# The key-value sums of pairs 0 to 7, with the exponentials as the stationary operand

## The chip, the cores and the metric

The kernel runs on one core of one Trainium2 chip. The metric is device time in microseconds, lower is better. Three runs of the kernel before gave 1171.79, 1172.33 and 1173.0 us; the median, 1172.33 us, is the time before.

In the profile the engines are called PE (matrix unit), PEld (its weight load, which overlaps PE), DVE (vector), ACT (scalar, activations), POOL (general purpose) and SP (queue of transfers).

## The reference

An attention with a feature map (8 batches, 8 heads, 576 positions, 64 values each) feeds a two-layer network. What is computed:

```python
def phi(x):
    proj = np.einsum('bhsd,df->bhsf', x, w_phi)                 # 64 -> 128 features
    proj = proj - np.max(np.abs(proj), axis=-1, keepdims=True)
    return np.concatenate([np.exp(proj), np.exp(-proj)], axis=-1)  # 256 features
q_p, k_p = (phi(q), phi(k))
kv = np.einsum('bhsf,bhsd->bhfd', k_p, v)
z = np.sum(k_p, axis=2)
num = np.einsum('bhsf,bhfd->bhsd', q_p, kv)
den = np.einsum('bhsf,bhf->bhs', q_p, z)[..., None] + 1e-06
attn = num / den
x = attn.transpose(0, 2, 1, 3).reshape(4608, 512)
h = x @ w_in                                                     # 512 -> 2048
out = np.maximum(0.01 * h, h) @ w_out                            # 2048 -> 512
```

All of it is fp32. The part that the change touches is `kv` and `z`: for each head a sum over the 576 positions of the 256 exponentials of a key times the 64 values of that position, and of the exponentials alone.

## The kernel before

**Pairs.** The 64 heads are worked on in 32 pairs. A pair has a key phase (projection, largest absolute value, subtraction, two exponentials, key-value sums) and a query phase (the same for the queries, then the product with the sums, then the division). A pair's 576 positions are taken in 5 chunks: four of 128 positions and one of 64, which sits on partitions 64 to 127.

**Two precisions.** Pairs 0 to 7 use plain fp32 matmuls. Each plain fp32 matmul of the program appears in the trace as two MATMUL records and two LDWEIGHTS records. Pairs 8 to 31, and the two layers of the network, split each operand in a high and a low part and use three faster matmuls in place of one (the type is F32R); these are one record each.

**Key-value sums of pairs 0 to 7.** For each chunk and each of the two heads one matmul has the 66 columns of the values as the stationary operand (64 values and two columns of ones, tile `rv`) and the 256 exponentials of the chunk as the moving operand (tile `e` in `first_k_phase`, `ek` in `k_phase`). The five chunks add up in one PSUM bank, `kvp`, 66 partitions by 2 x 256. The query phase wants the sums the other way round, features on the partitions. So the bank is copied to SBUF by ACT (`kvs`, L480 and L327, where the helper at L68 records it), turned by four transposes on PE into another bank (`kvt`, L485 and L333), and copied from there to `kvh` by two ACT copies: the 64 sums, and the column of `z` spread over 64 columns (L487 and L488, L336 and L337).

**Stages.** Pairs 0 and 1, then 2 and 3, run through `first_k_phase` (L445), then their queries through `first_q_phase` (L508) in three units of columns. Pairs 4 to 7 run through `k_phase` (L219) and `q_phase`, between matmuls of the network's layers for the first two blocks of 256 tokens (`layer1` L607, `layer2` L622). Meanwhile the weights of the two layers come in, 32 pieces, and DVE, ACT and POOL split them (`load_weights`, L170 to L200). From pair 8 on, attention of the next batches runs between the layers of the blocks before. The last blocks have layers alone.

**What sets the order.** The program gives each piece a priority, and a scheduler at build time, which plays the program through with its own idea of each instruction's duration, writes a fixed order for each engine. On the chip each engine takes its instructions in that order, and a waiting instruction holds back all behind it on its engine. PSUM banks come in four groups: `a` (3), `c` (1), `h` (2), `acc` (2). The sums of pairs 0 to 3 stand in `h`, those of pairs 4 to 7 in `c`, and all turned sums in `c`.

Of the kernel before, what the change touches and what calls it, by code (L numbers as in the profile page):

```python
# [45 lines left out]
def attention_moe_kernel(ctx: ExitStack, tc: tile.TileContext, q, k, v, w_phi, w_in, w_out, out):  # L46
# [171 lines left out]

    def k_phase(i):  # L219
# [62 lines left out]
        def chunk(c):  # L282
# [3 lines left out]
            if nat:  # L286
                nc.scalar.activation(ek[r, :, 0:F], pmk[r, 2 * s : 2 * s + 2], AF.Exp)
                nc.scalar.activation(ek[r, :, F:256], pmk[r, 2 * s : 2 * s + 2], AF.Exp, scale=-1.0)
                for j in range(2):
                    kv_mm(j, rv[r, 4 * j + c if c < 4 else 8 + j], ek[r, j], first=c == 0, last=c == 4)  # L290
                return
# [32 lines left out]
        if nat:  # L324
            load_v(i + 1)
        kvs = st([P, 2, 256], F32, "kk", "kvs").rearrange("p a (b f) -> p a b f", b=2)[0:66]
# [7 lines left out]
        if i < NN:  # L334
            kvh = st([P, 2, 2, P], F32, "kvh")
            nc.scalar.copy(kvh[:, :, :, 0:64], kvtv[:, :, :, 0:64])  # L336
            nc.scalar.copy(kvh[:, :, :, 64:P], kvtv[:, :, :, 64:65].broadcast_to([P, 2, 2, 64]))  # L337
            kvs_of[i] = kvh, None
        else:
            kvh = st([P, 2, 2, P], F32R, "kvh")  # L340
            kvl = st([P, 2, 2, P], F32R, "kvl")
            zb = kvtv[:, :, :, 64:65].broadcast_to([P, 2, 2, 64])
            copy_("kvh", kvh[:, :, :, 0:64], kvtv[:, :, :, 0:64])
            copy_("kvh", kvh[:, :, :, 64:P], zb)
            nc.vector.tensor_tensor(kvl[:, :, :, 0:64], kvtv[:, :, :, 0:64], kvh[:, :, :, 0:64].bitcast(F32), op=ALU.subtract)
            nc.vector.tensor_tensor(kvl[:, :, :, 64:P], zb, kvh[:, :, :, 64:P].bitcast(F32), op=ALU.subtract)
            kvs_of[i] = kvh, kvl
# [97 lines left out]
    def first_k_phase(i):  # L445
# [7 lines left out]
        for g in range(3):  # L453
# [18 lines left out]
            for s in range(w):  # L472
                c = 2 * g + s
                for j in range(2):
                    nc.tensor.matmul(kvp[0:66, 256 * j : 256 * j + 256], lhsT=rv[r, 4 * j + c if c < 4 else 8 + j],  # L475
                                     rhs=e[r, 2 * s + j].rearrange("p t f -> p (t f)"),
                                     start=c == 0 and j == 0, stop=c == 4, skip_group_check=True)
                yield
        kvs = st([P, 2, 256], F32, "kk", "kvs").rearrange("p a (b f) -> p a b f", b=2)[0:66]
# [247 lines left out]
```

## Time and profile before

| | before |
|---|---|
| median of 3 runs | 1172.33 us (1171.79 to 1173.0) |
| the profiled execution's own time | 1170.85 us |
| span of its trace | 1169.1 us |
| granted PE clock | 1.00 of full speed in the whole |
| busy: PE, PEld, DVE, ACT, POOL | 98%, 88%, 64%, 73%, 56% |

The span is what the trace shows from the first instruction to the last; 1.75 us of the execution lie outside. "Busy" of PE is taken from modelled ends of overlapping matmuls, so the pace of matmuls is better read from the starts of two groups that follow each other than from the length of one.

### The profile page before, as it was taken

How to read it: one execution, taken by the hardware profiler on the slowest of the kernel's cores; microseconds unless marked ns; L12 is line 12 of the kernel's file. 1: busy time of each engine (PE TensorE's matmuls, PEld its weight loads, DVE VectorE, ACT ScalarE, POOL GpSimd, SP SyncE). 2: the span in 40 equal slices, each digit the busy share in tenths (PEclk: the TensorE clock that was granted, in tenths of full speed). 3: DMA queues.
4: the chain of work that ended last, by engine and by line, in shares of the span. 5: the costliest groups of instructions: out<-in, count | busy, mean ns of one | idle time of the engine just before them, and what ended most of it. 6: DMA issues, size and time to landing. Idle time of an engine off the chain costs nothing.

```text
span 1169.1 us, 21456 instructions
## 1 busy us (share of the span) xinstructions
PE 1144.0 (98%) x7496; PEld 1025.8 (88%) x7496; DVE 751.6 (64%) x1316; ACT 856.2 (73%) x2256; POOL 649.1 (56%) x702
## 2 busy tenths in 40 slices
PE   8899999999999999999999999999999999999998
PEld 5677778898998999989999999999999999999997
DVE  6878996677778777776787777757867675200000
ACT  5878786888887888878888788868888885433232
POOL 1451222567667676767666766767666665533232
PEclk9999999999999999999999999999999999999999
DMA  8425441211111111111111111101111100000000
GB/s 221 151 78 153 123 119 36 66 37 33 52 34 51 34 41 33 44 31 32 42 34 52 33 52 26 49 22 41 34 51 34 41 2 20 1 19 10 10 19 19
DMA packets 69980, 57.87 MB, mean 50 GB/s; under 512 B 52208, under 2 KB 53488, under 8 KB 69872
## 3 DMA queue, kind: packets, MB, share of 16 engines
q1 hardware_dynamic: 67120, 55.78, 16.9%
q8 instruction: 59, 0.97, 0.4%
q10 hardware_dynamic: 2752, 0.72, 0.3%
q14 instruction: 49, 0.40, 0.1%
HBM read 46.27 MB, written 9.44 MB: 48 GB/s over the span
## 4 chain that ended last, share of the span: by engine, by line
PE 73%; DVE 12%; ACT 8%; issue 3%; DMA 2%; SPq 1%; POOL 1%; DVEq 0%; ACTq 0%; POOLq 0%
PE h L610 9%; PE h L613 9%; PE h L611 9%; PE acc L632 9%; PE acc L630 9%; PE acc L631 9%; PE c L241 6%; PE a L418 2%; PE a L423 2%; PE a L264 2%; PE a L420 2%; DVE tq L395 1%; DVE ql L189 1%; DMA m<-m 1%; PE h L475 1%
## 5 line engine op out<-in xcount | busy, mean ns | idle before, releaser
L73 POOL TENSOR_TENSOR gl<-g,gh 128x256 fp32r<-128x256 f32 x288 | 234.8, 819 | 321.4 <-ACT gh L68 242.4
L610 PE MATMUL h<-xh,w0h 128*128 128x256 f32 x1088 | 277.1, 282 | 2.8 <-ACT g L617 1.3
L611 PE MATMUL h<-xh,w0l 128*128 128x256 f32 x1088 | 275.5, 280 | 0.0
L610 PEld LDWEIGHTS h<-xh,w0h 128*128 128x128 f32 x1088 | 204.6, 188 | 13.6 <-ACT g L617 2.8
L630 PE MATMUL acc<-w1h,gh 128*128 128x512 f32 x544 | 214.2, 394 | 0.1
L631 PE MATMUL acc<-w1l,gh 128*128 128x512 f32 x544 | 213.4, 392 | 0.0
L611 PEld LDWEIGHTS h<-xh,w0l 128*128 128x128 f32 x1088 | 204.5, 188 | 8.4
L632 PE MATMUL acc<-w1h,gl 128*128 128x512 f32 x544 | 203.3, 394 | 0.2 <-POOL gl L73 0.2
L613 PE MATMUL h<-xl,w0h 128*128 128x256 f32 x1088 | 189.6, 280 | 0.1
L617 ACT ACTIVATE g<-h 128x256 f32<-128x256 f32 x288 | 108.6, 381 | 98.1 <-PE h L613 79.7
L73 POOL TENSOR_TENSOR ql<-eq,qh 128x576 fp32r<-128x576 f32 x96 | 144.4, 1517 | 41.9 <-DVE qh L409 29.1
L68 ACT CAST gh<-g 128x256 fp32r<-128x256 f32 x288 | 115.2, 402 | 67.8 <-PE acc L631 66.1
L613 PEld LDWEIGHTS h<-xl,w0h 128*128 128x128 f32 x1088 | 155.1, 188 | 1.2 <-POOL xl L73 0.5
L73 POOL TENSOR_TENSOR kpl<-ek,kph 128x512 fp32r<-128x512 f32 x72 | 99.6, 1383 | 75.4 <-ACT kph L68 65.4
L70 DVE COPY o<-acc 128x512 f32<-128x512 f32 x17 | 11.7, 686 | 162.8 <-DMA out_dram<-o 77.9
L632 PEld LDWEIGHTS acc<-w1h,gl 128*128 128x128 f32 x544 | 99.7, 188 | 15.9 <-POOL gl L73 0.6
L630 PEld LDWEIGHTS acc<-w1h,gh 128*128 128x128 f32 x544 | 102.3, 188 | 12.3 <-ACT gh L68 0.4
L631 PEld LDWEIGHTS acc<-w1l,gh 128*128 128x128 f32 x544 | 102.3, 188 | 11.3
L294 ACT ACTIVATE ek<-pmk,m4n 128x128 f32<-128x128 f32 (+1 forms) x240 | 90.2, 392 | 12.1 <-DVE m4n L278 8.5
L295 ACT ACTIVATE ek<-pmk,m 128x128 f32<-128x128 f32 (+1 forms) x240 | 89.6, 390 | 8.0 <-DVE m L272 7.0
L269 DVE TENSOR_TENSOR pmk<-a,pmk 128x256 f32<-128x256 f32 (+1 forms) x120 | 49.4, 419 | 58.4 <-ACT pmk L68 56.9
L409 DVE TENSOR_REDUCE qh<-eq 128x576 fp32r<-128x576 f32 x96 | 69.0, 750 | 24.0 <-ACT eq L403 21.7
(186 smaller groups left out, 2399.5 us busy)
## 6 DMA issues: line engine op xcount, KB each, us to landing
out_dram<-o SPq DMA_DIRECT2D x36, 256.0 KB, 2.1
rv<-in_v_dram SPq DMA_DIRECT2D x28, 320.0 KB, 3.6
rq<-in_q_dram SPq DMA_DIRECT2D x28, 288.0 KB, 3.0
rk<-in_k_dram SPq DMA_DIRECT2D x27, 288.0 KB, 2.8
ring<-in_w_in_dram SPq DMA_DIRECT2D x9, 512.0 KB, 3.6
f<-in_w_out_dram SPq DMA_DIRECT2D x7, 512.0 KB, 3.7
f<-in_w_in_dram SPq DMA_DIRECT2D x7, 512.0 KB, 3.7
ring<-in_w_out_dram SPq DMA_DIRECT2D x5, 512.0 KB, 4.3
```

What stands on the lines that cost most here:

```text
L68: nc.scalar.copy(o, i)
L73: (nc.vector if pick(key) == "v" else nc.gpsimd).tensor_tensor(o, a, b, op=op)
L241: nc.tensor.matmul(kvp[0 : lt.shape[1], 256 * j : 256 * j + 256], lhsT=lt, rhs=rt, start=first and j == 0, stop=last, skip_group_check=True)
L294: nc.scalar.activation(ek[r, j, 0:F], pmk[r, h], AF.Exp, bias=m4n[r, h : h + 1])
L295: nc.scalar.activation(ek[r, j, F:256], pmk[r, h], AF.Exp, scale=-1.0, bias=m4[r, h : h + 1])
L610: nc.tensor.matmul(ph, lhsT=weight(0, "h", ft)[:, d * P : d * P + P], rhs=xh[d], start=d == 0, stop=False)
L611: nc.tensor.matmul(ph, lhsT=weight(0, "l", ft)[:, d * P : d * P + P], rhs=xh[d], start=False, stop=False)
L613: nc.tensor.matmul(ph, lhsT=weight(0, "h", ft)[:, d * P : d * P + P], rhs=xl[d], start=False, stop=d == NP - 1)
L617: nc.scalar.activation(g, ph, AF.Prelu, alpha=0.01)
L630: nc.tensor.matmul(a, lhsT=gh[:, ts], rhs=weight(1, "h", ft), start=ft == 0, stop=False)
L631: nc.tensor.matmul(a, lhsT=gh[:, ts], rhs=weight(1, "l", ft), start=False, stop=False)
L632: nc.tensor.matmul(a, lhsT=gl[:, ts], rhs=weight(1, "h", ft), start=False, stop=ft == NFT - 1)
```

## The change

In pairs 0 to 7 the two operands of the key-value matmuls change places. For each chunk and head there are now two matmuls, one for each half of the 256 features: the 128 exponentials are stationary and the 66 columns of `rv` move (`kv_nat`). The sums come out with the features on the partitions, four blocks of 66 columns in one bank. So the copy to `kvs` and the four transposes are gone, and the two copies to `kvh` read the bank of the sums itself (`kv_copy`). Pairs 8 to 31 keep their code.

```diff
+    def kv_nat(kvp, rv, r, c, ek):
+        for j in range(2):
+            for t in range(2):
+                n = 66 * (2 * j + t)
+                nc.tensor.matmul(kvp[:, n : n + 66], lhsT=ek(j, t), rhs=rv[r, 4 * j + c if c < 4 else 8 + j],
+                                 start=c == 0 and n == 0, stop=c == 4, skip_group_check=True)
+
+    def kv_copy(kvp, kvh):
+        kv = kvp[:, 0:264].rearrange("p (a b f) -> p a b f", a=2, b=2)
+        nc.scalar.copy(kvh[:, :, :, 0:64], kv[:, :, :, 0:64])
+        nc.scalar.copy(kvh[:, :, :, 64:P], kv[:, :, :, 64:65].broadcast_to([P, 2, 2, 64]))
+        return kvh
...
@@ k_phase: chunk
-                for j in range(2):
-                    kv_mm(j, rv[r, 4 * j + c if c < 4 else 8 + j], ek[r, j], first=c == 0, last=c == 4)
+                kv_nat(kvp, rv, r, c, lambda j, t: ek[r, j, F * t : F * t + F])
...
@@ k_phase: end
         if nat:
             load_v(i + 1)
+            kvs_of[i] = kv_copy(kvp, st([P, 2, 2, P], F32, "kvh")), None
+            yield
+            return
...
@@ first_k_phase
             for s in range(w):
-                c = 2 * g + s
-                for j in range(2):
-                    nc.tensor.matmul(kvp[0:66, 256 * j : 256 * j + 256], lhsT=rv[r, 4 * j + c if c < 4 else 8 + j],
-                                     rhs=e[r, 2 * s + j].rearrange("p t f -> p (t f)"),
-                                     start=c == 0 and j == 0, stop=c == 4, skip_group_check=True)
+                kv_nat(kvp, rv, r, 2 * g + s, lambda j, t: e[r, 2 * s + j, t])
                 yield
-        kvs = st([P, 2, 256], F32, "kk", "kvs").rearrange("p a (b f) -> p a b f", b=2)[0:66]
-        copy_("kvs", kvs, kvp[0:66].rearrange("p (a b f) -> p a b f", a=2, b=2))
-        kvt = pt("c")
-        kvtv = kvt[:, 0:264].rearrange("p (a b f) -> p a b f", a=2, b=2)
-        for j in range(2):
-            for t in range(2):
-                nc.tensor.transpose(kvtv[:, j, t], kvs[:, j, t], ident[0:66, 0:66])
-        kvh = first_kvh(i)
-        nc.scalar.copy(kvh[:, :, :, 0:64], kvtv[:, :, :, 0:64])
-        nc.scalar.copy(kvh[:, :, :, 64:P], kvtv[:, :, :, 64:65].broadcast_to([P, 2, 2, 64]))
-        kvs_of[i] = kvh, None
+        kvs_of[i] = kv_copy(kvp, first_kvh(i)), None
         yield
```

With other instructions the scheduler writes another order. Two places of it follow. (L223 is the new matmul, L228 and L229 the two copies to `kvh`; in the changed program L439 has become L448, L463 L472, L287 and L288 have become L300 and L301, and L617 has become L612. The tiles `f_79` and `f_82` hold keys and values of pairs 2 and 3, `f_80` those of pair 1, `f_81` and `ring` exponentials, `rk` the keys and `rv` the values of pair 0.)

PE in the first 25 us, key-value sums of pairs 0 and 1 and projections of pairs 2 and 3, before:

```order
L475 MATMUL h<-ring,rv 66x256 x4
L475 MATMUL h<-ring,f_80 66x256 x4
L439 MATMUL acc<-bd,f_79 128x256 x2
L439 MATMUL a<-bd,f_82 128x256 x4
L475 MATMUL h<-f_81,rv 66x256 x3
L475 MATMUL h<-ring,f_80 66x256 x2
L475 MATMUL h<-f_81,rv 66x256
L475 MATMUL h<-ring,f_80 66x256 x2
L475 MATMUL h<-ring,rv 66x256 x2
L439 MATMUL acc<-bd,f_79 128x256 x3
L439 MATMUL a<-bd,f_82 128x256
L475 MATMUL h<-f_81,f_80 66x256 x2
```

The same place in the changed program, from the last sums of chunks 2 and 3 on:

```order
L223 MATMUL h<-rv,f_81 128x66 x3
L223 MATMUL h<-f_80,ring 128x66 x4
L223 MATMUL h<-rv,ring 128x66 x4
L223 MATMUL h<-f_80,f_81 128x66 x4
L448 MATMUL acc<-bd,f_79 128x256
L448 MATMUL a<-bd,f_82 128x256 x2
L448 MATMUL acc<-bd,f_79 128x256 x2
L448 MATMUL a<-bd,f_82 128x256 x3
L448 MATMUL acc<-bd,f_79 128x256
L223 MATMUL h<-f_79,ring 128x66 x8
```

Before, six of the ten projections of pairs 2 and 3 stood after the first eight sums of pairs 0 and 1; now one stands among these sums and nine behind the last of them.

ACT after the last exponentials of pair 4 (`w0h` and `kvl` belong to the weights, `g` is the activation of layer 1), before:

```order
L186 ACTIVATE ql<-f_79 128x512
L68 COPY kvs<-c 66x512
L287 ACTIVATE ek<-pmk 128x2x128
L288 ACTIVATE ek<-pmk 128x2x128
L287 ACTIVATE ek<-pmk 128x2x128
L288 ACTIVATE ek<-pmk 128x2x128
L287 ACTIVATE ek<-pmk 128x2x128
L288 ACTIVATE ek<-pmk 128x2x128
L68 CAST w0h_92<-ql 128x512
L191 ACTIVATE kvl<-f_79 128x512
L617 ACTIVATE g<-h 128x256
L336 COPY kvh<-c 128x4x64
```

The same place in the changed program:

```order
L300 ACTIVATE ek<-pmk 128x2x128
L301 ACTIVATE ek<-pmk 128x2x128
L300 ACTIVATE ek<-pmk 128x2x128
L301 ACTIVATE ek<-pmk 128x2x128
L228 COPY kvh<-c 128x4x64
L229 COPY kvh<-c 128x4x64
L300 ACTIVATE ek<-pmk 128x2x128
L301 ACTIVATE ek<-pmk 128x2x128
L68 CAST w0h_92<-ql 128x512
L191 ACTIVATE kvl<-f_79 128x512
L612 ACTIVATE g<-h 128x256
```

The copy that needs pair 4's finished sums stood ahead of the six exponentials of pair 5; the copies that now need them stand behind six of these, and `g` has the two copies to `kvh` ahead of it, which it had behind it.

More of the change, by code (lines that the diff above doesn't have):

```diff
@@ L333, in k_phase @@
                 nc.tensor.transpose(kvtv[:, j, t], kvs[:, j, t], ident[0:66, 0:66])
-        if i < NN:
-            kvh = st([P, 2, 2, P], F32, "kvh")
-            nc.scalar.copy(kvh[:, :, :, 0:64], kvtv[:, :, :, 0:64])
-            nc.scalar.copy(kvh[:, :, :, 64:P], kvtv[:, :, :, 64:65].broadcast_to([P, 2, 2, 64]))
-            kvs_of[i] = kvh, None
[L339 to L347, printed above, removed]
+        kvh = st([P, 2, 2, P], F32R, "kvh")
+        kvl = st([P, 2, 2, P], F32R, "kvl")
+        zb = kvtv[:, :, :, 64:65].broadcast_to([P, 2, 2, 64])
+        copy_("kvh", kvh[:, :, :, 0:64], kvtv[:, :, :, 0:64])
+        copy_("kvh", kvh[:, :, :, 64:P], zb)
+        nc.vector.tensor_tensor(kvl[:, :, :, 0:64], kvtv[:, :, :, 0:64], kvh[:, :, :, 0:64].bitcast(F32), op=ALU.subtract)
+        nc.vector.tensor_tensor(kvl[:, :, :, 64:P], zb, kvh[:, :, :, 64:P].bitcast(F32), op=ALU.subtract)
+        kvs_of[i] = kvh, kvl
         yield
@@ L472, in first_k_phase @@
             for s in range(w):
-                c = 2 * g + s
-                for j in range(2):
-                    nc.tensor.matmul(kvp[0:66, 256 * j : 256 * j + 256], lhsT=rv[r, 4 * j + c if c < 4 else 8 + j],
-                                     rhs=e[r, 2 * s + j].rearrange("p t f -> p (t f)"),
-                                     start=c == 0 and j == 0, stop=c == 4, skip_group_check=True)
-                yield
-        kvs = st([P, 2, 256], F32, "kk", "kvs").rearrange("p a (b f) -> p a b f", b=2)[0:66]
-        copy_("kvs", kvs, kvp[0:66].rearrange("p (a b f) -> p a b f", a=2, b=2))
-        kvt = pt("c")
-        kvtv = kvt[:, 0:264].rearrange("p (a b f) -> p a b f", a=2, b=2)
-        for j in range(2):
-            for t in range(2):
-                nc.tensor.transpose(kvtv[:, j, t], kvs[:, j, t], ident[0:66, 0:66])
-        kvh = first_kvh(i)
-        nc.scalar.copy(kvh[:, :, :, 0:64], kvtv[:, :, :, 0:64])
-        nc.scalar.copy(kvh[:, :, :, 64:P], kvtv[:, :, :, 64:65].broadcast_to([P, 2, 2, 64]))
-        kvs_of[i] = kvh, None
+                kv_nat(kvp, rv, r, 2 * g + s, lambda j, t: e[r, 2 * s + j, t])
+                yield
+        kvs_of[i] = kv_copy(kvp, first_kvh(i)), None
         yield
```

## The prediction

> **What bounds the kernel now.** First the page's head, then the busy time by stage (columns: stretch in us, its length, busy us and instructions of each engine, granted clock, share of the transfer engines).
>
> ```profile
> span 1169.1 us, 21456 instructions
> PE 1144.0 (98%) x7496; PEld 1025.8 (88%) x7496; DVE 751.6 (64%) x1316; ACT 856.2 (73%) x2256; POOL 649.1 (56%) x702
> 5.00:41.00 36.00, 34.75 (x161) 24.56 (x162) 28.02 (x49) 24.27 (x51) 8.43 (x8) 1.00 0.75 213
> 41.00:82.00 41.00, 35.35 (x187) 27.73 (x186) 36.37 (x71) 31.54 (x77) 24.87 (x29) 1.00 0.33 99
> 82.00:100.00 18.00, 16.74 (x94) 12.75 (x94) 11.72 (x25) 12.89 (x32) 2.89 (x4) 1.00 0.53 142
> 100.00:180.00 80.00, 77.22 (x430) 61.98 (x429) 77.43 (x141) 64.76 (x149) 18.84 (x21) 1.00 0.43 123
> 180.00:400.00 220.00, 216.39 (x1448) 195.40 (x1447) 158.59 (x273) 178.55 (x483) 134.10 (x143) 1.00 0.15 41
> 400.00:980.00 580.00, 578.54 (x3998) 535.12 (x3997) 423.00 (x731) 479.39 (x1299) 392.76 (x394) 1.00 0.13 36
> ```
>
> From 180 us on PE sets the pace: 1.5 us idle in 580. Until 41 us (pairs 0 to 3) it does nearly so too. From 41 to 82 us (queries of pairs 0 to 3) PE is idle 5.7 us and DVE, at 36.4 of 41, is the tighter engine. From 100 to 180 us both are at 97%. There the question is whether PE waits for the weights that DVE splits. The waits of PE over the whole span answer it (columns: us in total, times, longest):
>
> ```profile
> PE h L610 <- ACT g L617: 3.4, 7, 1.3
> PE c L241 <- DVE kst L309: 1.7, 4, 0.9
> PE c L552 <- ACT dn L556: 1.6, 2, 1.3
> PE a L530 <- DVE pm L524: 1.6, 4, 0.5
> PE c L485 <- ACT kvs L68: 0.8, 1, 0.8
> PE h L610 <- POOL w1h L195: 0.3, 1, 0.3
> ```
>
> PE has one wait of 0.3 us on a weight tile. So the full DVE of 100 to 180 us is not what PE waits for, and PE work saved from 82 us on is time saved, as long as no other wait grows. From 41 to 82 us it may be lost to DVE.
>
> **The matmuls.** What a group costs PE is read from its start to the start of the next group, in the timeline:
>
> ```profile
> 27.82 0.41 PE L485 MATMUL c<-ident,kvs 66*128 66x66 f32 x4
> 28.07 1.89 PE L475 MATMUL h<-f,f 128*66 128x256 f32 x8
> 77.25 2.00 PE L552 MATMUL c<-eq,f 128*128 128x64 f32 x16
> 79.08 0.70 PE L376 MATMUL a<-rq,bd 128*128 128x288 f32 x2
> 80.73 1.89 PE L552 MATMUL c<-eq,f 128*128 128x64 f32 x16
> 82.43 0.36 PE L610 MATMUL h<-qh,w0h 128*128 128x256 f32 x1
> 83.70 3.62 PE L241 MATMUL c<-ek,rv 128*66 128x256 f32 x16
> 87.15 0.65 PE L376 MATMUL a<-rq,bd 128*128 128x288 f32 x2
> ```
>
> Old: 16 records in 87.15 - 83.70 = 3.45 us, 0.216 us each. A pair has 5 chunks x 2 heads x 2 records = 20, so 4.31 us.
>
> New: twice as many matmuls, 40 records a pair, each with 128 stationary columns (there were 66) and 66 moving (there were 256). No such matmul of kv is in the trace, but L552 has plain fp32 records of 128 stationary and 64 moving columns: 1.83 us / 16 = 0.114 and 1.70 / 16 = 0.106 us. I take their mean, 0.110: 4.40 us a pair. The moving side falls to a quarter, the pace only to half. Over 8 pairs this is +0.7 us, with the two rows as ends -0.5 to +2.0 us. A far lower end is the transposes, which also have 128 stationary and 66 moving columns, at 0.25 / 4 = 0.062 us; L552 is nearer, since it multiplies.
>
> [...]
>
> Gone: four transposes a pair, 0.25 us, so -2.0 us over 8 pairs. **PE work in all: +0.7 - 2.0 = -1.3 us**, half of it in pairs 0 to 3 and half in pairs 4 to 7.
>
> **The copies.** ACT loses the copy to `kvs`; the two copies to `kvh` keep their size.
>
> ```profile
> L68 ACT COPY kvs<-c 66x512 f32<-66x512 f32 x4 | 2.3, 578 | 2.1 <-PE c L241 2.1
> L68 ACT COPY kvs<-h 66x512 f32<-66x512 f32 x4 | 2.2, 589 | 0.0
> ```
>
> That is 8 copies, 4.5 us of ACT, by itself worth nothing: ACT is at 31.5 of 41 and 64.8 of 80 where they ran. If ACT had no room, they would be worth up to 4.5 us. What counts is two waits around them. No transfer changes in number.
>
> **The first wait, pairs 0 to 3.** The first row below is PE held by the copy, with the next products behind the transposes.
>
> ```profile
> 38.45 0.47 PE L485 MATMUL c<-ident,kvs 66*128 66x66 f32 x4 [0.80 <-ACT kvs L68]
> 11.40 1.89 PE L475 MATMUL h<-ring,rv 128*66 128x256 f32 x8
> 15.71 1.89 PE L439 MATMUL a<-bd,f 128*128 128x256 f32 x8
> 17.44 1.46 PE L475 MATMUL h<-f,rv 128*66 128x256 f32 x6
> 15.91 0.69 DVE L463 TENSOR_REDUCE m<-acc 128x4 f32<-128x512 f32 x1 [1.50 <-PE acc L439]
> 16.71 0.69 DVE L465 TENSOR_TENSOR pm<-acc,m 128x512 f32<-128x512 f32 x1
> 21.14 0.63 ACT L470 ACTIVATE ring<-pm 128x512 f32<-128x512 f32 x1 [1.18 <-issue]
> 21.39 0.98 DVE L189 SCALAR_TENSOR_TENSOR ql<-ring,ql 128x512 int32<-128x512 int32 x1
> 21.68 0.61 ACT L471 ACTIVATE ring<-pm 128x512 f32<-128x512 f32 x1
> ```
>
> The 0.8 us go, and with half of the PE work (-0.65) pairs 0 to 3 would end 1.45 us sooner. Against it stands the new order of projections. Nine of the ten for pairs 2 and 3 now come after all sums of pairs 0 and 1: from the first sum at 11.4 us, 40 new matmuls of 0.22 and one projection of 0.43 (four of them, 8 records, take 17.44 - 15.71 = 1.73) give 20.6 us, so DVE starts on pair 2 at about 21 instead of 15.9. Behind the projection that starts it, PE still has 8 others, 3.4 us; the chain that the first new sum of pair 2 waits for is 0.69 + 0.69 + 0.63 + 0.61 = 2.6 us. So it is just covered, unless a piece of weight work on DVE (the 0.98 us of L189) stands in between. And what PE gains meets DVE, which has 4.6 us of slack from 41 to 82. Bounds: -1.45 us (all kept) to +2.1 us, the reduction twice and the subtraction once (2.06 us) that DVE had done by 21 us and now has not, if none of it is caught up. I take -0.9: most is kept, DVE eats a third.
>
> **The second wait, pair 4.** On ACT the copy to `kvs` blocks for 2.14 us, with six exponentials of pair 5, then the weight pieces, then `g`, behind it; PE's next layer 1 waits for `g`, whose bank it needs.
>
> ```profile
> 89.90 0.58 ACT L68 COPY kvs<-c 66x512 f32<-66x512 f32 x1 [2.14 <-PE c L241]
> 90.39 0.42 ACT L287 ACTIVATE ek<-pmk 128x256 f32<-128x256 f32 x1
> 92.24 0.60 ACT L68 CAST w0h<-ql 128x512 fp32r<-128x512 f32 x1
> 92.75 0.67 ACT L191 ACTIVATE kvl<-f 128x512 int32<-128x512 uint32 x1
> 93.31 0.37 ACT L617 ACTIVATE g<-h 128x256 f32<-128x256 f32 x1
> 93.74 0.39 PE L610 MATMUL h<-qh,w0h 128*128 128x256 f32 x1 [1.26 <-ACT g L617]
> ```
>
> Now the six exponentials (92.24 - 90.39 = 1.85 us) fit in the 2.14 us of waiting. The two copies to `kvh` and two exponentials, about 1.2 us, then take the place of `kvs` and the six, 0.5 + 1.85 us, ahead of the weights and `g`: `g` starts some 1.2 us sooner, and PE's 1.26 us nearly vanish. Bounds: -1.26 to 0, if another engine's wait takes its place. I take -1.2. Pairs 4 to 7 add their half of the PE work, -0.65.
>
> **Sum:** -0.9 - 1.2 - 0.65 = -2.75 us on the profiled execution of 1170.85 us (1.75 us more than its span). The median is 1.5 us above that execution; applied to it, 1172.33 - 2.75 = **1169.6 us**.
>
> **What the sum can't hold.** From 180 us on, the work is unchanged but its order is written anew. There PE idles 3.6 us until 400 and 1.5 until 980, in single waits such as this one:
>
> ```profile
> 355.22 0.68 PE L241 MATMUL c<-kst,vhl 128*64 128x256 f32 x4 [0.89 <-DVE kst L309]
> ```
>
> Two or three such waits more or fewer give the forecast its own spread, +-2.5 us: 1167.1 to 1172.1.
>
> **The rivals.**
>
> *Nothing comes of it.* Pairs 0 to 3 end sooner but DVE sets the end of 41 to 82 us, and the 1.2 us at 93 us become a wait for the maxima of pair 4's queries. Left are -0.65 us of PE work: 1171.7. For it speaks DVE's 36.4 of 41; against it that PE has no large wait between 100 and 180 us.
>
> *The moving side sets the pace.* If a new record cost what a transpose of that shape does, 0.062 us, a pair's sums would take 2.5 us instead of 4.31: -14.6 us over 8 pairs, and -16.6 with the transposes. Pairs 0 to 3 would lose most of theirs to DVE, so I count half: 1172.3 - 8.3 - 1.2 = 1162.8. Against it stand both L552 groups. [...]
>
> *Slower: the late projections.* DVE begins on pair 2 five us later and is the tight engine until 82 us. If the lost 2.06 us are not caught up, and weight work in front of the exponentials of pairs 2 and 3 holds PE 1 us at each of two groups, the first stage ends 2.06 + 2 = 4.1 us later; with -1.85 from pair 4 on this is +2.2: 1174.5. It decides from the point where DVE's delay exceeds the 1.45 us that pairs 0 to 3 gain. For it: DVE waits 1.5 us for a projection already. Against: DVE's 4.6 us of slack, and idle time elsewhere before 41 us.
>
> **Chances.** Forecast 0.50, nothing 0.22, moving side 0.06, late projections 0.17, some other growth of waits 0.05. What a measurement of this kernel can tell from no change is about 0.2%, 2.3 us, so the bounds are 1170.0 and 1174.7. A bit over half of the forecast's half (0.28), the moving side and a little of "nothing" through the order's spread (0.06) are faster: 0.40. Slower are half of the late projections, other waits and an unlucky order: 0.18. Within: 0.42. The range, 1165.5 to 1175.0, leaves out the moving side and the worst of the late projections.
>
> **What would show it.** In the changed profile: groups of L223 at 0.106 to 0.114 us a record (0.062: the moving side). No wait of PE on a copy near 38 us. PE's last sums of pairs 2 and 3 done a microsecond or more before 38.45 us, where PE now leaves its wait for the copy. `L612` at about 92 us, with the wait of PE's next L605 below 0.3 us. The start of the last L552-like group of 64 columns (L547) before 80.7 us; if it is later, the late projections won. PE busy from 180 to 980 us within 2 us of 795. The prediction is wrong if a group of L223 runs at another pace, or if PE's idle time after 180 us moves by more than 3 us.

## The result and the profile after

The change made the kernel slower: 1181.18 us (four runs, 1177.29 to 1185.54), against 1172.41 us for the kernel before on the same chip. The ratio is 1.0072, with a 95% interval of 1.0057 to 1.0086, so about 8.8 us were lost where 2.75 were to be gained. The profiled execution took 1177.29 us, 6.4 more than the one of before. Four single runs far above all others of their kernel (1605.58 us of the kernel before, 1250.02, 3997.18 and 1444.07 us in the experiments) count in no figure of this document.

First the head of the page and the busy time by stage after the change (columns as in the prediction).

```profile
span 1175.5 us, 21728 instructions
PE 1145.8 (97%) x7624; PEld 1040.1 (88%) x7624; DVE 763.5 (65%) x1316; ACT 853.9 (73%) x2248; POOL 650.0 (55%) x702
41.00:82.00 41.00, 33.86 (x175) 26.66 (x174) 36.36 (x72) 32.18 (x77) 24.89 (x29) 1.00 0.34 99
82.00:100.00 18.00, 18.00 (x135) 16.63 (x135) 14.99 (x30) 14.21 (x34) 3.55 (x5) 1.00 0.56 170
180.00:400.00 220.00, 213.34 (x1424) 192.27 (x1423) 158.34 (x273) 176.88 (x478) 135.28 (x140) 1.00 0.15 41
400.00:980.00 580.00, 576.19 (x3956) 530.13 (x3955) 432.11 (x725) 473.76 (x1287) 384.73 (x389) 1.00 0.13 36
```

From 82 to 100 us PE now has no idle time at all (1.3 us before). But from 180 to 980 us, where the instructions are the same as before, PE is busy 789.5 us instead of 794.9.

Some of the waits of PE over the whole span, after (columns: us in total, times, longest):

```profile
PE a L525 <- DVE pm L519: 2.2, 2, 1.6
PE c L254 <- DVE kst L321: 2.0, 3, 1.3
PE c L547 <- ACT dn L551: 1.7, 1, 1.7
PE acc L627 <- POOL gl L73: 1.5, 2, 1.2
PE a L427 <- DVE pmk L282: 1.2, 1, 1.2
```

The first and third of these rows lie in the stage before 82 us. The other three are waits of layer and attention work, on the keys (`kst`), the low half of the layer's activation (`gl`) and the maximum of a key (`pmk`); `gl` and `pmk` held PE for no row of this size before.

Now the places the prediction named, in the timeline of after (columns: start, length, engine, line, operation, tiles, shape, count; in brackets the wait ahead of a row and what ended it).

```profile
11.34 1.90 PE L223 MATMUL h<-rv,ring 128*128 128x66 f32 x16
13.07 1.95 PE L223 MATMUL h<-f,ring 128*128 128x66 f32 x16
14.85 0.39 PE L223 MATMUL h<-rv,f 128*128 128x66 f32 x2
28.03 0.41 PE L223 MATMUL h<-f,ring 128*128 128x66 f32 x2 [0.91 <-issue]
37.16 0.66 PE L525 MATMUL a<-ident,pm 128*128 128x128 f32 x4
81.55 1.90 PE L547 MATMUL c<-eq,f 128*128 128x64 f32 x16
92.36 0.36 ACT L612 ACTIVATE g<-h 128x256 f32<-128x256 f32 x1
93.29 0.28 PE L605 MATMUL h<-qh,w0h 128*128 128x256 f32 x1
```

A record of the new sums costs 1.73 / 16 = 0.108 and 1.78 / 16 = 0.111 us. PE waits 0.91 us ahead of the row at 28.03. The profile names nothing that ended this wait; the exponentials on ACT just ahead of it end at 27.94, and they hang on the late projections. PE has done the sums of pairs 2 and 3 by 37.16 us, when the row behind them starts. The kernel before had done its own sums by 36.95, with only the transposes behind the wait for the copy:

```profile
36.95 0.70 PE L439 MATMUL acc<-bd,ks 128*128 128x256 f32 x2
```

So the 1.3 us between 37.16 and the end of that wait, 38.45, are not a gain. The last 64-column group of the first stage starts at 81.55 us, 0.82 later than before: by 82 us nothing of a gain is left. `g` starts 0.95 us sooner and the next L605 does not wait for it.

How far ahead is the changed kernel? I compared, from the two traces, when each has the same amount of PE work still ahead of it. By this count, which depends a little on what a record is taken to cost, the changed kernel leads by 0.9 us at 41 us, lies 0.5 behind at 82, leads by 2.3 at 120, 2.7 at 200 and 2.2 at 220. Then it is 1.1 behind at 400, 5.2 behind at 500, 3.5 at 900, and 6.3 from 980 us to the end. So the loss arises behind 220 us, most of it by 500 us, and it is larger than what was gained up to there.

The lead of 2.7 us at 200 us is not all it seems. The same group of layer 1 and the same DVE group of the attention beside it, before:

```profile
204.20 0.64 PE L613 MATMUL h<-xbl,w0h 128*128 128x256 f32 x4
205.15 0.76 DVE L269 TENSOR_TENSOR pmk<-a,pmk 128x256 f32<-128x256 f32 x2
```

And after:

```profile
201.12 0.64 PE L608 MATMUL h<-xbl,w0h 128*128 128x256 f32 x4
205.34 0.76 DVE L282 TENSOR_TENSOR pmk<-a,pmk 128x256 f32<-128x256 f32 x2
```

PE has run 3.1 us ahead with layer work, but the chain of DVE on the next keys is not ahead (0.2 us behind). PE's lead is work done early, which it lacks later as cover for that chain.

What an order can cost shows near 490 us. POOL splits the activation of layer 1 into `gl`, and PE's layer 2 needs two such pieces. After the change the second `gl` stands behind a piece of `vhl` and one of `ring`:

```profile
489.12 0.73 POOL L73 TENSOR_TENSOR gl<-g,gh 128x256 fp32r<-128x256 f32 x1
489.81 1.83 POOL L73 TENSOR_TENSOR vhl<-rv,vhl 128x512 fp32r<-128x512 f32 x2
491.72 0.79 POOL L73 TENSOR_TENSOR ring<-ring,dn 128x288 f32<-128x288 f32 x1
492.47 0.72 POOL L73 TENSOR_TENSOR gl<-g,gh 128x256 fp32r<-128x256 f32 x1
493.24 0.73 PE L627 MATMUL acc<-w1h,gl 128*128 128x512 f32 x2 [1.18 <-POOL gl L73]
```

Before, the same pieces stood with both `gl` ahead of `ring` and `vhl`, and PE did not wait (other rows of POOL stand between these):

```profile
481.35 0.74 POOL L73 TENSOR_TENSOR gl<-g,gh 128x256 fp32r<-128x256 f32 x1
483.43 0.73 POOL L73 TENSOR_TENSOR gl<-g,gh 128x256 fp32r<-128x256 f32 x1
485.51 0.80 POOL L73 TENSOR_TENSOR ring<-ring,dn 128x288 f32<-128x288 f32 x1
486.27 1.84 POOL L73 TENSOR_TENSOR vhl<-rv,vhl 128x512 fp32r<-128x512 f32 x2
486.17 0.71 PE L632 MATMUL acc<-w1h,gl 128*128 128x512 f32 x2
```

This work has nothing to do with the change. The scheduler, which plays the program through with its own durations, came out at other choices. That is the theory the experiments start from: **the new order of the unchanged work behind 220 us is what costs.** The rivals: the new arithmetic costs it (matmuls, operands, clock), or the shifted instruction stream does.

### The profile page after: what moved, and what is told of

It reads as the page before. It is cut to its first block, busy times and chain, and to the rows that moved or that the text cites. A ratio compares the mean times of both kernels' runs of the same rounds, so it can differ in the third digit from the quotient of the medians.

```text
span 1175.5 us, 21728 instructions
## 1 busy us (share of the span) xinstructions
PE 1145.8 (97%) x7624; PEld 1040.1 (88%) x7624; DVE 763.5 (65%) x1316; ACT 853.9 (73%) x2248; POOL 650.0 (55%) x702
## 4 chain that ended last, share of the span: by engine, by line
PE 76%; DVE 8%; ACT 8%; issue 3%; POOL 2%; DMA 2%; SPq 0%; ACTq 0%; DVEq 0%; POOLq 0%
PE h L605 10%; PE h L608 9%; PE h L606 9%; PE acc L627 9%; PE acc L626 9%; PE acc L625 9%; PE c L254 5%; PE a L427 2%; PE a L277 2%; PE a L432 2%; PE a L429 2%; PE h L223 2%; DVE tq L404 1%; PE a L387 1%; PE a L388 1%
## 5 line engine op out<-in xcount | busy, mean ns | idle before, releaser
L605 PE MATMUL h<-xh,w0h 128*128 128x256 f32 x1088 | 276.9, 282 | 2.1 <-ACT g L612 1.0
L605 PEld LDWEIGHTS h<-xh,w0h 128*128 128x128 f32 x1088 | 204.5, 188 | 11.1 <-ACT g L612 2.2
L612 ACT ACTIVATE g<-h 128x256 f32<-128x256 f32 x288 | 107.8, 380 | 99.1 <-PE h L608 80.1
```

Of the source, the lines that this page charges most:

```text
L605: nc.tensor.matmul(ph, lhsT=weight(0, "h", ft)[:, d * P : d * P + P], rhs=xh[d], start=d == 0, stop=False)
L612: nc.scalar.activation(g, ph, AF.Prelu, alpha=0.01)
```

## Experiments: order or arithmetic

A table of instructions for each engine can fix the order at build time. Each neighbour in the table gets a dependency on the one ahead of it on the same engine, which adds no wait between engines:

```diff
+        for line in table:                 # one line per engine
+            for earlier, later in zip(line, line[1:]):
+                tc.add_manual_dep(ins[later], ins[earlier].name, nosync, reason="order")
```

I call the order that the scheduler gives the changed kernel order A, and that of the kernel before order B. Behind the first fifth of the program they share only 74% of the neighbours on PE, 56% on ACT, 58% on DVE and 53% on POOL.

**Old arithmetic, order A behind 210 us.** The sums of pairs 0 to 7 are computed as before; only the order of what follows is that of the changed kernel.

> The mirror of the first: the arithmetic of the kernel before, its own order up to its 14th product with xbl (210.0 us), and from there what is left in the changed kernel's order. Order theory: the loss without the change, 1172.4 + 8.5 = 1181 us, between 1178 and 1185, with single runs some us apart as in the changed kernel. Arithmetic theory: 1172 to 1173. A broken fit: 1174 to 1178.

Measured: 1181.05 us, ratio 1.0072 (1.006 to 1.0084). That is the whole loss, without one instruction of the change. The busy time from 220 to 500 us, for before, after and this kernel in turn (same columns as above):

```profile
220.00:400.00 180.00, 176.59 (x1208) 160.85 (x1207) 136.40 (x236) 150.56 (x406) 119.05 (x120) 1.00 0.16 44
400.00:500.00 100.00, 99.75 (x695) 92.43 (x694) 73.69 (x133) 84.91 (x233) 68.23 (x70) 1.00 0.16 43
```

```profile
220.00:400.00 180.00, 173.92 (x1191) 158.09 (x1190) 137.56 (x237) 150.65 (x404) 117.81 (x115) 1.00 0.16 44
400.00:500.00 100.00, 98.06 (x663) 88.54 (x662) 76.81 (x126) 80.30 (x223) 66.58 (x70) 1.00 0.15 40
```

```profile
220.00:400.00 180.00, 174.25 (x1180) 158.62 (x1179) 135.55 (x234) 148.78 (x401) 118.82 (x118) 0.99 0.16 44
400.00:500.00 100.00, 98.05 (x660) 88.40 (x659) 75.56 (x126) 79.73 (x219) 65.68 (x69) 1.00 0.14 36
```

PE idles 3.7 us in this stretch before, 8.0 after, and 7.7 with the old arithmetic in order A. Idle time holds some 4 us of the loss. The rest lies within what counts as busy: PE's busy time in the whole span rose by 1.8 us (1144.0 to 1145.8), although the records cost no more. I did not break that part down further.

**New arithmetic, order B all through.** Where the two differ, the new matmuls take the places of the old ones.

> All of the changed kernel's arithmetic in the order of the kernel before from the first instruction to the last: two new matmuls stand in the place of each old one, the copies to kvh where they stood, the copies to kvs and the transposes are gone. This takes the late projections away too. Order theory: 1172.4 less 1.3 us of PE work and at most the two waits (0.9 + 1.2): 1169 to 1171 us. Arithmetic theory: 1179 to 1182.

Measured: 1173.98 us, ratio 1.0006 (0.9998 to 1.0015), 12 runs. The loss is gone, but so is the gain. The timeline shows where the two removed waits went:

```profile
26.64 1.97 PE L223 MATMUL h<-f,ring 128*128 128x66 f32 x16 [0.61 <-issue]
45.12 0.70 PE L547 MATMUL h<-eq,f 128*128 128x256 f32 x2 [1.12 <-ACT eq L532]
96.25 4.70 PE L223 MATMUL c<-rv,ek 128*128 128x66 f32 x32 [1.76 <-ACT kvl L191]
```

The wait at 45.12 has a counterpart before:

```profile
44.50 0.70 PE L552 MATMUL h<-eq,f 128*128 128x256 f32 x2 [0.90 <-ACT eq L537]
```

Times here are counted from the first sum, 12.19 us in this trace and 11.40 before. PE loses 0.61 us at 26.64 to a wait that was not there before and that the profile does not explain. It arrives only 0.4 us sooner at the queries' exponentials, which come 0.2 us sooner, so the wait there grows from 0.90 to 1.12. At the second place PE passes `g` without a wait, arrives sooner at the next pair's sums and waits 1.76 us there, behind a weight piece on ACT. What it waits for had not become faster.

**New arithmetic and order A to 214 us, order B behind.** This puts the early part of the changed kernel, with its lead of 2.2 us, ahead of the old tail.

> All of the changed kernel's arithmetic. Every engine issues the changed kernel's own order up to its 15th product with xbl (214.1 us in its trace) and from there what is left in the order of the kernel before; the orders are forced by dependencies between neighbours on one engine, which add no wait between engines. Order theory (the sums themselves give what was predicted, about -2.2 us by 220 us, and the +8.5 us of PE idle time from 220 to 980 us come from the order alone): 1170.2 us, between 1168.5 and 1172, and PE busy again as before from 400 to 980 us (579 of 580). Arithmetic theory (the new sums themselves bring the loss, whatever the order behind them): 1179 to 1182. A fit of head and tail that the swap breaks: 1174 to 1178.

Measured: 1177.67 us, ratio 1.0044 (1.0025 to 1.0063), but spread from 1172.26 to 1184.7. The tail runs parallel to that of before. So the order was right as a cause, yet this kernel should then have been at 1170 to 1173 and only its best run was. The runs' times follow their mean granted clock: 1172.26 at 1.000, 1184.7 at 0.990, some 1.2 us for 0.001. A second cause was at work, and it has its own section below.

**Which half of the change flips the order?** Pairs 4 to 7 alone changed, then pairs 0 to 3 alone, each with the order that the scheduler gives it.

```diff
 first_k_phase (pairs 4 to 7 alone):
-                kv_nat(kvp, rv, r, 2 * g + s, lambda j, t: e[r, 2 * s + j, t])
+                for j in range(2):
+                    nc.tensor.matmul(kvp[0:66, 256 * j : 256 * j + 256], lhsT=rv[r, ...], rhs=e[r, 2 * s + j]...)
 k_phase (pairs 0 to 3 alone):
-                kv_nat(kvp, rv, r, c, lambda j, t: ek[r, j, F * t : F * t + F])
+                for j in range(2):
+                    kv_mm(j, rv[r, ...], ek[r, j], first=c == 0, last=c == 4)
```

> Only pairs 4 to 7 have the new sums, pairs 0 to 3 the old; the scheduler writes the order of everything anew. By the predicted terms alone 1172.4 - 0.65 - 1.2 = 1170.5 us. Order theory: the terms hold until about 180 us, and the time is that plus what the newly written order happens to cost, anything from 1167 to 1183; PE idle time behind 220 us tells which. If the loss hangs on the sums of pairs 4 to 7: 1179 to 1182, and if it hangs on those of pairs 0 to 3 or on their late projections: 1170 to 1171.

> Only pairs 0 to 3 have the new sums; the scheduler is free, and from 220 us on it writes the order of the kernel before, instruction for instruction. Order theory: no loss behind 220 us; the time is that of the kernel before but for what pairs 0 to 3 bring, predicted -0.9 (with late projections +2.1), and what the lead table of the changed kernel shows at 82 us, +0.5: 1172 to 1174 at full clock. If the loss came from the sums of pairs 0 to 3 or their late projections: 1178 or more.

Measured: pairs 4 to 7 alone 1187.95 us, 1.0129 (1.0115 to 1.0142); pairs 0 to 3 alone 1181.4 us, 1.0078 (1.0048 to 1.0109). From 220 us on the first has order A instruction by instruction, the second has order B. So the sums of pairs 4 to 7 flip the order. But the second kernel is slow in order B as well, which the theory of the order did not allow: even its runs at a clock of 1.000 took 1176.6 to 1180. (In the traces it is 4.4 us behind before at 83 us, from its first stage, and 11.9 us at the end.) And the first is 7 us above the full change. Something else costs several microseconds in both. They have in common that they differ from before by 64 PE records, half of the change's 128 (7624 - 7496); that is the third cause.

## Experiments: the granted clock

In some runs with the new sums of pairs 0 to 3 the clock falls while PE is working. The first kernel with the order exchanged (order A to 214 us, then B), by windows of 3.4 us:

```profile
26.20:29.60 3.40, 2.09 (x17) 1.93 (x17) 3.12 (x7) 2.62 (x5) 0.93 (x1) 1.00 0.25 100
29.60:33.00 3.40, 3.40 (x16) 3.21 (x15) 3.21 (x8) 3.01 (x7) 0.00 (x0) 0.50 0.00 0
33.00:36.40 3.40, 3.40 (x18) 3.40 (x18) 2.16 (x4) 1.49 (x3) 1.01 (x1) 0.50 0.00 0
36.40:39.80 3.40, 3.40 (x14) 3.04 (x14) 0.65 (x2) 0.00 (x0) 0.00 (x0) 0.50 0.77 251
```

From 29.6 to 39.8 us the clock is 0.50, with PE busy all the time. The falls last 3.41, 6.83 or 10.24 us, one to three times 3.41: this one lasts 10.24, and one in order B (from 98.86 us, below) 6.83. Why they come in these lengths no run shows. Ahead of this fall PE is busy 2.09 of 3.40 us, at a clock of 1.00.

The new sums move only 66 columns a record. To test whether that is the reason, four of the five chunks stream 128 columns instead of 66; the 62 extra columns are the neighbouring values, and their sums are not used.

```diff
-                n = 66 * (2 * j + t)
-                nc.tensor.matmul(kvp[:, n : n + 66], lhsT=ek(j, t), rhs=rv[r, 4 * j + c if c < 4 else 8 + j],
+                n = 128 * (2 * j + t)
+                w = 128 if c < 4 else 66
+                x = 66 * (4 * j + c if c < 4 else 8 + j)
+                nc.tensor.matmul(kvp[:, n : n + w], lhsT=ek(j, t), rhs=rv[r].rearrange("p a f -> p (a f)")[:, x : x + w],
```

Two kernels that switch from order A to B already at 201 us, the second with 128 columns; then the changed kernel in its own order with 128 columns; then order B all through with 128 columns.

> The first run again with the seam at a better place: the changed kernel's own order up to its 13th product with xbl (201.1 us in its trace), where both kernels have done the same work but for one instruction on each side, and from there the order of the kernel before. Order theory: the lead of 2.4 to 2.7 us that the changed kernel has there is kept to the end, 1172.4 - 2.5 = 1170 us in the runs whose mean granted clock is 1.000; the wait of 2.1 us at the seam of the first run (PE L605 for ACT g) is gone. Each 0.001 of clock below that costs 1.2 us, as in the first run's list (1172.3 at 1.000, 1184.7 at 0.990). [...]

> The same order and arithmetic, but four of the five chunks stream 128 columns (the 66 that are wanted and 62 of the slot beside them, into columns of the bank that nothing reads) past the stationary exponentials instead of 66. [...] Rival, the falls come from PE's waits or from the chip, not from the columns: clocks and times as in the run before. Rival, 128 columns do cost PE time: groups of 16 records take over 1.85 us instead of 1.73, and the time grows by 3 us or more at full clock.

> The changed kernel in exactly its own order, with the 128 columns. Order theory: the loss behind 220 us stays, 1179 to 1183 us, whatever the clock. [...] If the falls of the clock were the main loss of the changed kernel, this is 1170 to 1173.

> The changed kernel's arithmetic in the order of the kernel before throughout, with 128 streamed columns: the three side effects (order, clock, fetches) are taken out, and what is left is the change itself. The predicted sum for it, PE work alone: -1.3 us; with the two waits up to -2.75. The trace of the same order with 66 columns gives less, since behind pairs 0 to 3 and behind pair 4 PE waits for DVE and ACT instead: -1.0 to +0.5. So 1171.5 to 1173.5 us, and no run under a clock of 0.998.

Measured, in this order: 1178.17 us, 1.0042 (1.0021 to 1.0064), from 1173.42 to 1185.08; 1173.51 us, 1.0004 (0.9994 to 1.0014); 1181.92 us, 1.0069 (1.0054 to 1.0084); 1173.52 us, 1.0004 (0.9995 to 1.0012).

The only difference of the first two is the width, and it takes away 4.7 us of the median and the spread (mean clocks of 0.989 to 1.000 in the first, of 0.998 to 1.000 in the second). The same place in the second:

```profile
26.20:29.60 3.40, 2.67 (x20) 2.44 (x20) 3.31 (x7) 2.98 (x6) 1.13 (x1) 1.00 0.26 104
29.60:33.00 3.40, 3.40 (x32) 3.37 (x32) 3.21 (x8) 3.28 (x8) 0.00 (x0) 1.00 0.00 0
```

The second stretch is now at full clock and holds 32 records instead of 16. Since PE also waits a little less ahead of it (2.67 us busy instead of 2.09), one pair of traces does not settle that the width is the cause; the lists of runs say more. Of 61 runs of kernels with 66 columns in pairs 0 to 3 (this change among them), 18 had a mean clock of 0.995 or less, which is an estimate of some 11 us or more at half clock (0.005 of some 1175 us, divided by a half). Of 36 runs with 128 columns none had, and of some 137 runs with the old sums in pairs 0 to 3 none. In order B the falls come with 66 columns too, only less: 8 of 12 runs had 0.996 to 0.998, and the profiled one has half clock from 98.86 to 105.68 us, in the midst of the sums of pair 5 and behind them. With 128 columns in the same order all 11 runs had 0.999 or more.

Single falls of 3.41 us are not peculiar to the narrow sums. They stand in traces of the old sums (at 362.2 us with order A; at 39.0 us in before with 32 records more, a kernel below) and of 128 columns (at 232.2 us with 32 records more, also below). PE had been idle in part there: ahead of the one at 39.0 us it was busy 2.1 of 3.41 us, and in the 4 us in which the other two begin 2.66 (360 to 364 us) and 2.55 us (230 to 234 us). Behind a stretch in which PE was busy throughout a fall was seen only with 66 columns, as in pairs 0 to 3 alone:

```profile
36.28:39.70 3.42, 3.42 (x30) 3.28 (x30) 2.44 (x5) 1.57 (x4) 2.53 (x3) 1.00 1.00 382
39.70:43.11 3.41, 3.41 (x13) 2.85 (x12) 1.16 (x2) 2.29 (x6) 1.55 (x2) 0.50 0.59 203
```

Another stretch full of narrow records has no fall behind it: in the changed kernel PE is busy all 9.00 us from 11 to 20 us, with 78 records, and the clock is 1.00 there and in the 4 us behind. So these rows do not give the whole rule.

And 128 columns cost hardly more than 66. From start to start a record of 128 columns takes 0.111 to 0.112 us (in order B, groups of 16 start at 12.59, 14.37 and 16.16 us) against 0.108 to 0.111 with 66. Over the 256 wide records that is an estimate of 0.8 us at most.

What follows for the loss: the changed kernel in its own order keeps its 8 to 9 us with 128 columns, so the clock is not the cause of its median. It explains single runs (1185.54 us at 0.994). And order B with 128 columns, in which neither order nor clock disturbs, is the change by itself: +0.5 us (-0.6 to +1.4) with up to 0.8 us for the width in it, not -2.75.

The first two kernels were to keep the early lead and come out near 1170 us at full clock; neither did. Why was the lead not worth anything in the second? At its switch PE waits for the chain of DVE that was not ahead:

```profile
207.20 0.50 PE L279 MATMUL a<-wq,ks 128*128 128x256 f32 x2 [1.27 <-DVE pmk L284]
```

From there on it is parallel to before to within 1.3 us.

## Experiments: where the instruction stream is fetched

What is left is why half of the change is slow in order B. The page of before has 59 packets of kind "instruction" in a queue `q8`, 0.97 MB in all, 16 KB each, so one for about 127 of PE's 7496 records. In its trace 98 to 151 records of PE lie between one and the next, but 0 to 60 of DVE, 21 to 65 of ACT and 8 to 35 of POOL; from this I take the packets for PE's own instructions. They come in all through the run, from 27.68 to 1148.96 us, and a packet took 0.88 to 1.47 us, 1.16 in the median. After the change, with 128 records more, there are 60.

My theory was that a fetch that meets an output transfer may delay it; where it meets one depends on how many records lie ahead. The whole change adds 128, about one packet's worth and one block in what follows, and leaves the meeting points where they were, counted in records of the unchanged work; each half adds 64. So I added small matmuls at the start, on a block of zeros of `bd`, into a bank that nobody reads. They run while PE waits for its first data, and the first projection then starts at 5.56 us instead of 5.45.

```diff
+    spare = pt("c")
+    for _ in range(32):
+        nc.tensor.matmul(spare[0:16, 0:16], lhsT=bd[0:64, F : F + 16], rhs=bd[0:64, F : F + 16], start=True, stop=True)
```

32 of them are 64 records. First: the kernel before with 64 more; pairs 0 to 3 alone with 64 more; pairs 4 to 7 alone with 64 more.

> The kernel before in exactly its own order, with 64 small matmul records (16 columns of a block of zeros, results unused) that PE works off before its first projection, while it waits for the first transfers until 5.45 us. What is under test: PE's instructions are fetched in blocks of 16384 bytes by the queue that also carries the outputs (one fetch per 128 matmul records, some 1.1 us each in the traces), and in the two kernels with the new sums in four pairs only, 64 records more than before, the fetches fall half a block away from where they fall in the kernel before and in the changed kernel (128 records more, one whole block). There the outputs landed late at other places (3.5, 4.3, 5.1 us instead of 2.0) and PE's waits grew. Fetch theory: half a block costs this order some 5 to 6 us whatever is computed: 1176 to 1180 us. Rival, the fetches don't matter and the two kernels were late for what they compute: 1171 to 1173.5.

> The kernel with the new sums in pairs 0 to 3 only, in exactly its own order, and the 64 small records at the start: now a whole block more than before. Fetch theory: 1172.5 to 1175 us in runs at full clock (1176.6 to 1180.0 without them), and the outputs land late where they did in the kernel before. Rival: no change, 1177 to 1181.

> The kernel with the new sums in pairs 4 to 7 only, in exactly its own order, which behind 220 us is that of the changed kernel, and the 64 small records at the start. Fetch theory: 1179.5 to 1183 us, as the changed kernel, instead of 1188: the order's 8 us stay and the fetches' 6 us go. Rival: no change, 1186 to 1190.

Measured: 1176.44 us, 1.004 (1.0027 to 1.0052); 1175.15 us, 1.0029 (1.0012 to 1.0047); 1177.2 us, 1.0038 (1.0025 to 1.0051). The kernel before loses 3.5 us by idle instructions that cost 0.11 us where they stand (5.56 - 5.45). The two halves gain: pairs 0 to 3 from 1181.4 (runs at a clock of 0.999 or more from 1176.4 to 1181.3 without the records, from 1172.8 to 1176.9 with them), pairs 4 to 7 from 1187.95. The control, a whole block of 128 idle records in front of the kernel before, was not run.

Arithmetic and order of the kernel before and of its variant with 64 more are the same, so an instruction can be compared with itself. Before: an ACT copy into the output tile, a matmul behind it, and from the view of the transfers of 226.8 to 231.2 us the outputs (size, then us from issue to landing):

```profile
229.00 0.58 ACT L68 COPY o<-h 128x512 f32<-128x512 f32 x1
246.44 0.65 PE L241 MATMUL c<-kph,vhl 128*66 128x256 f32 x4 [0.35 <-DVE kvl L346]
out_dram<-o SPq DMA_DIRECT2D x2, 256.0 KB, 2.0
```

With 64 records more (transfers of 227.6 to 232 us):

```profile
232.03 0.59 ACT L68 COPY o<-h 128x512 f32<-128x512 f32 x1 [2.11 <-DMA out_dram<-o]
249.84 0.67 PE L244 MATMUL c<-kph,vhl 128*66 128x256 f32 x4 [1.76 <-DVE kvl L349]
q8 instruction: 1, 0.02, 2.5%
out_dram<-o SPq DMA_DIRECT2D x1, 256.0 KB, 4.3
```

There a fetch (`q8`) falls into the output transfer, which takes 4.3 us instead of 2.0. The tile `o` comes free late, ACT waits 2.11 us for it, and what is queued behind the copy reaches PE as a wait of 1.76 us. (The first expectation speaks of one queue for fetches and outputs. The page has the fetches in a queue of their own, `q8`, and the view of 226.8 to 231.2 us, where two outputs of before land, has packets of `q1` alone, 333 of them. What slows the output where a fetch falls into it, no view shows.)

This is one place of one trace, but the packets of all the traces can be counted. In the eleven kernels that are whole blocks of records apart, before and after among them, 3 or 4 of the 36 outputs overlap in time with a fetch of PE. In the seven others, 6 to 10 do. Every output that took over 4 us overlaps one, but not every overlap goes with a late output: in the trace of before the four took 2.0, 2.8, 3.8 and 4.5 us and the 32 others 2.0 to 3.4, and after the change the three took 2.7 to 3.8 and the others 2.0 to 3.8.

Then the other shifts, in both orders. The kernels in order B are before with 32 and 96 more, those in order A the changed kernel with 128 columns (to keep the clock out) with 32 and 96 more.

> The kernel before in its own order with 32 small records at the start, a quarter of a fetch block. The order is the same, so what changes is only where PE's fetches fall among the transfers. Fetch theory: anything between the time at no shift (1172.9) and a little over that at half a block (1176.4): 1172 to 1178 us, at full clock, with the outputs landing late at other places. If the order alone decides: 1172 to 1173.5.

> As the run before with 96 small records, three quarters of a block: 1172 to 1178 us by the fetch theory, 1172 to 1173.5 if the order alone decides.

> The changed kernel in exactly its own order, with 128 streamed columns (so without the falls of the clock, 1182.3 us) and 32 small records at the start. Two theories of the loss behind 220 us. The order itself is worse: it stays some 5 us or more above the kernel before wherever the fetches fall, 1178 to 1188. Order and fetches together: the order is as good as the other and only meets the fetches at bad places, so that a quarter of a block more or less brings it to 1170 to 1174.

> As the run before with 96 small records: 1178 to 1188 us if the order itself is worse, 1170 to 1174 in this run or the one before if it is the meeting of order and fetches.

Measured: 1173.99 us, 1.0005 (0.9996 to 1.0013); 1176.16 us, 1.0025 (1.0016 to 1.0033); 1186.29 us, 1.0115 (1.0101 to 1.0128); 1190.8 us, 1.0144 (1.0127 to 1.016), above what was expected. The clock stayed out of the third only in part: its four runs had 0.996 or 0.997, which at 1.2 us for 0.001 is 4 to 5 us at most. All medians together, in us:

| records added, beyond whole blocks of 128 | order B | order A |
|---|---|---|
| 0 | 1172.9 (before) | 1181.9 (128 columns) |
| 32 | 1174.0 | 1186.3 |
| 64 | 1176.4 | 1188.0 (pairs 4 to 7 alone) |
| 96 | 1176.2 | 1190.8 |

Order A is worse at every shift, by 9 to 15 us, and by 7 or more if all that the clock can have cost in its second row is taken off; the two orders are not two draws of one lottery. Within an order the shift is worth 3.5 us (B) or some 9 us (A). Before and after stand in the same, best row, and few outputs meet a fetch in either (4 and 3 of 36). So the fetches can hardly be a large part of their difference, though in another order the few meetings fall on other work; the shift of 64 records is why each half of the change alone looked worse than it should (1181.4 against 1175.15 us with 64 more, 1187.95 against 1177.2).

One number stays partly open: pairs 4 to 7 alone with 64 more stands in order A and in the first row, and took 1177.2 us, 5 us below the table's 1181.9. The two traces can be compared at the same product of layer 1 (the third of `xbl` behind 198 us): it starts at 217.93 us in the kernel with 128 columns and at 213.67 in this one. Of the 6.3 us between the ends of their spans (1180.8 and 1174.5), 4.3 are there by this product. So most of the difference lies ahead of the part in which order A loses; why, no run shows.

## Why the prediction was wrong

The forecast was 1169.6 us, within 1165.5 to 1175.0; it came to 1181.18, above the range.

**The step that failed is "What the sum can't hold".** The prediction saw that the order behind 180 us is written anew and gave that +-2.5 us, two or three single waits. It is worth +8.4 us (7.0 to 9.9, the ratio of the old arithmetic in order A applied to 1172.4). I had counted waits of the kind that the trace of before has. But a new order is not the old one with a few waits moved: between 26% and 47% of the neighbours differ, and a chain can be late in many places by a little. The prediction's own test says it: PE busy from 180 to 980 us was to be within 2 us of 795 and is 789.5; PE's idle time there grew by 5.4 us, and more than 3 was to mean that it is wrong. "Some other growth of waits", at 0.05, is the case that came.

**The matmuls: right.** 0.108 and 0.111 us a record against 0.110. The moving side as the pace (0.062) is refuted, and more sharply by the 128 columns, which cost 0.111 to 0.112: with 128 stationary columns the step from 66 to 128 moving columns adds at most 0.004 us to a record, that to 256 some 0.1 (the projections of L439, 1.73 / 8 = 0.216). What holds the narrow records at 0.11 us, no run shows; the transposes, with 128 stationary columns too, went at 0.062 us.

**The first wait: right at its place, wrong in its worth.** PE no longer waits for the copy. But that its last sums were done a microsecond before 38.45 us, the sign that the prediction gave, could not tell anything: before had done them by 36.95. From the first sum to the last 64-column group it is 69.33 us before (80.73 - 11.40), 69.24 with the new arithmetic in order B (that group starts at 81.43 there) and 70.21 in order A (81.55 - 11.34). So 0.1 us was gained or 0.9 lost, where 1.45 were counted and 0.9 taken. PE waited for producers that were hardly sooner: in order B at 26.64 us and for `eq` at 45 us, in order A at 28.03 us. In order A DVE started on pair 2 at 21.61 us, as the prediction said, and a weight piece stood in the chain behind it, the condition that the prediction named. "Nothing comes of it" named this mechanism (DVE sets the end of 41 to 82 us, busy 36.4 of 41 us in both traces), and at 0.22 it was too low. By the prediction's mark of 80.7 us the late projections had won; with 0.82 us at 82 us it was a small victory, and the 4.1 us of that rival did not come.

**The second wait: right at its place, wrong in its worth.** `g` at 92.36 (92 was said) and no wait behind it. In order B the time came back at the next sums, as 1.76 us with 66 columns and 0.92 with 128; in order A it stayed as PE's lead, without DVE's chain being ahead, and was lost where that chain was needed.

**The sum.** -2.75 us became +0.5 (-0.6 to +1.4, the width's estimate of 0.8 at most included) with the order held and the clock undisturbed. The terms of PE's work and of the two waits were sized at PE. They should have been followed to the next thing that PE needs from another engine; each of them ended there.

## What to carry to other kernels

Where a scheduler at build time writes the order, a local change has two prices: its own, and that of the new order of everything else. The second can be the larger one (here +8.4 against +0.5 us), has no sign that the change gives away, and is measured by holding the order: the new arithmetic in the old order, and the old arithmetic in the new one. When a wait is taken away, find the next instruction whose producer was not made sooner; the gain ends there.

Before a difference of a few microseconds is put down to a change, count what it does to the number of instructions on the longest stream (64 idle records made the kernel before 3.5 us slower), and look at the granted clock of single runs where narrow matmuls follow each other for long: widening the moving side to 128 columns cost an estimate of 0.8 us at most here, and a mean clock of 0.995 or less came in 18 of 61 runs with 66 columns and in none of 36 with 128.

## What the runs showed of the hardware that was not expected

- The granted clock of PE halved while its rows showed it busy, for 3.41, 6.83 or 10.24 us at a time. A mean clock of 0.995 or less came in 18 of 61 runs with 128 stationary and 66 moving columns, in none of 36 with 128 moving columns and in none of some 137 with the old sums in pairs 0 to 3. The cost is some 1.2 us for 0.001 of the mean clock (1172.26 us at 1.000, 1184.7 at 0.990). Single falls of 3.41 us came without the narrow sums too, there where PE had been idle in part (busy 2.1 of 3.41 us ahead of the one at 39.0 us). How narrow the records have to be, and for how long, was not measured.
- Plain fp32 records with 128 stationary columns take 0.108 to 0.111 us with 66 moving columns and 0.111 to 0.112 with 128, against 0.216 with 256.
- Packets of kind "instruction" come in during the run, 59 of 16 KB in the kernel before, one for some 127 records of PE. Where one overlapped a 256 KB output, the output took 2.0 to 4.5 us before the change and up to 5.8 with 64 records more; without one it took 2.0 to 3.8 in the traces of before and after. And 64 records that cost 0.11 us by themselves made the kernel before 3.5 us slower (1176.44 against 1172.93).

What stays open: which of the many choices of order A cost most (the `gl` near 490 us is one, of 1.2 us), why its loss is in part inside PE's busy time, what the rule behind the falls of the clock is, and why pairs 4 to 7 alone with 64 more were 4.3 us ahead by 214 us. A repaired order, or one chosen among several for its time on the chip, was not tried.
